# Linear attention in front of two MLPs on one core: k and v of a head pair in one gapless load each

## The chip, the core and the metric

The kernel runs on one core of a Trainium2 chip. A core has five engines that run side by side and wait for each other by semaphores: TensorE (PE in the rows; its loads of the stationary operand are listed apart as PEld), VectorE (DVE), ScalarE (ACT), GpSimd (POOL) and SyncE (SP), which here only issues transfers. The transfers of all issuers run on the same 16 DMA engines. The metric is the time of one execution on the device, in microseconds.

## What is computed

```python
def _attn_ref(q, k, v, g_norm):                       # 4 x 8 heads, 576 rows, 64 columns
    kv = np.einsum('bhsd,bhse->bhde', k, v)           # 64 x 64 per head
    out = np.einsum('bhsd,bhde->bhse', q, kv)
    rms = np.sqrt(np.mean(out * out, axis=-1, keepdims=True) + 1e-06)
    return out / rms * g_norm
...
x = attn_out.transpose(0, 2, 1, 3).reshape(2304, 512)
h = x @ w_in            # 512 x 2048, then softplus, then @ w_out
...
h = x @ w_in2           # the same sizes, then leaky relu (0.01), then @ w_out2
```

k^T v of a head is a sum over all 576 rows, so the order in which the rows are taken doesn't matter as long as k and v are taken alike. All inputs and the output are float32.

## The kernel before

**Work and its order.** The 32 heads are taken as 16 units of two heads each (`unit`, four head pairs in each of four batches). Each step of the program is an `op` with a price for each engine that may do it; `Plan.run` gives every op an engine and a place in that engine's queue, at build time. The first 600 or so places are not planned but written out by hand in the table `FIRST` (a letter for the engine, E for TensorE, G for a transfer that ScalarE issues, and the number of the op); what follows the table is ordered by prices and due times. Each engine then works through its queue in order.

**Loads (`load`, L430).** For each unit q, k and v are loaded with 512 of their 576 rows, four rows of a head to a partition: 128 partitions x 2 heads x 256 elements, 256 KB, in runs of 1 KB. There are five buffers of each (`qa`, `ka`, `va`). The 64 rows that are left come once a batch for all heads: `kr` and `vr` with 64 partitions x 8 heads x 64, and `qr` in two halves. Those of the first batch are issued by ScalarE, the others by SP. The lower halves of `kr` and `vr` are set to zero once, on GpSimd, so that they can be multiplied with all 128 partitions.

**A unit (`T`, L460).** q and k are copied with the two heads side by side (`qp`, `kp`, L406 to L410, on ScalarE, VectorE or GpSimd). TensorE turns q in four transposes (`f_t`, L479; at the first unit of two also the left rows of q, L483), and multiplies k with v: four products of 128 x 128 over the rows (`f_kv`, L487) and a fifth over the left rows (`f_kvl`, L492). Both heads stand in k and in v, so a product of 128 columns holds the two wanted 64 x 64 blocks and two that are not wanted; a mask takes the blocks out (`f_m`, L505 on VectorE, L508 on ScalarE) into `kvm`. A product in fp32 is two loads of weights and two passes, as two records in the trace.

**Behind it.** `O` (L523) multiplies the turned q with `kvm` (L527, and L534 for the left rows of two units), `normal` (L558) makes the norm, `X` (L606) turns the result back (L612, L623) into `xy`. In between stand the decoding of the first MLP weights (`decode_pair`, `split_pair`) and the first plain products of the MLP (L984). The MLPs (L894, L1151, L1156 and what feeds them) fill the rest.

Of the kernel before, what the change touches and what calls it, by code (L numbers as in the profile page):

```python
# [21 lines left out]
class Plan:  # L22
# [13 lines left out]
    S7 E26 S0 S80 G6 S9 G5 S8 S1 G4 P40 S2 G3 D27 S85 E44 E42 S10 E32 S13 A82 S14 S15 A83 S11 A81 E29  # L36
    S24 D41 S12 D30 E45 S23 D28 D84 S38 S16 A90 E33 A31 S37 S19 E34 E46 D35 S39 D47 A36 D91 E69 A43 S17
    D87 E52 A88 S20 D48 D55 A86 E68 S18 A53 D89 P100 S22 A72 D54 A70 E102 S21 P101 E104 A92 D73 E57 D71
    S50 E60 E105 A58 S49 D103 A74 P56 D59 S51 A75 E106 D76 E61 S66 A107 D25 D78 S65 A108 E62 D79 E134
    S67 D77 A63 S110 D93 A64 E132 S109 A136 P166 E135 E116 A167 D94 P119 D95 A138 E168 D139 A117 D137  # L40
    E170 E171 A133 D118 P120 A169 E124 D96 A140 E172 E178 D97 A141 A173 E125 D142 A174 D145 A98 D144
    E126 E180 S131 E121 D127 E200 A179 D143 S129 P185 S113 A128 D186 A122 E198 D99 A123 S115 E182 A202
    P213 A199 S114 D181 E187 D203 A183 E201 S146 P212 E190 A204 E191 S111 D184 A321 S130 D205 D188 E192
    A206 S112 P236 E214 D189 E228 A207 D208 E216 P235 S175 A229 E217 S151 D211 D209 A215 A193 S176 E218
    E230 P262 D219 S177 E248 A194 D210 A231 E232 A324 S195 D220 S196 D322 E251 S197 E250 A254 A249 D325
    S222 E266 S245 A252 E264 E274 S225 D265 A233 E237 D255 D253 A147 E240 S227 E481 P263 A238 D234 S226
    A148 D149 E241 S221 A256 D150 P281 A257 S223 A275 E242 D258 S246 E267 A156 D261 S224 A243 D259 A239
# [120 lines left out]
def linear_attention_two_mlps(  # L168
# [32 lines left out]
    nc = tc.nc  # L201
# [178 lines left out]
    for t_ in ldr["k"] + ldr["v"]:  # L380
        nc.gpsimd.memset(t_[RL:], 0.0)
# [48 lines left out]
    def load(u):  # L430
        b, hp = unit(u)
        hs = slice(2 * hp, 2 * hp + 2)
        for nm, src in (("q", q), ("k", k), ("v", v)):
            def fn(e, nm=nm, src=src):
                nc.sync.dma_start(
                    out=lda[nm][u % NLD],
                    in_=src[b, hs, 0:4 * P, :].rearrange("h (p r) d -> p h r d", r=4),
                )

            op({"S": 0.73}, fn, (), [(nm, u % NLD)])  # L440
        if u % NPAIR:
            return
        e_ = "G" if b == 0 else "S"
        for nm, src in (("k", k), ("v", v)):
            def fn(e, nm=nm, src=src):
                (nc.scalar if e == "G" else nc.sync).dma_start(
                    out=ldr[nm][b % 2][:RL], in_=src[b, :, 4 * P:S, :].rearrange("h p d -> p h d")
                )

            op({e_: 0.58}, fn, (), [(nm + "r", b % 2)])  # L450
        for x in range(2):
            def fn(e, x=x):
                (nc.scalar if e == "G" else nc.sync).dma_start(
                    out=ldr["q"][b % 2][x * RL:(x + 1) * RL],
                    in_=q[b, NPAIR * x:NPAIR * (x + 1), 4 * P:S, :].rearrange("h p d -> p h d"),
                )

            op({e_: 0.29}, fn, (), [("qr", b % 2, x)])

    def T(u):  # L460
# [3 lines left out]
        for nm, dst in (("q", qp), ("k", kp)):  # L464
# [6 lines left out]
        kv = ps[p1][:, 2 * P:3 * P]  # L471
        ql, kl, vl = (ldr[nm][b % 2] for nm in "qkv")
# [4 lines left out]
        def f_t(e, j):  # L477
# [16 lines left out]
        for j in range(2):  # L494
            n = 2 * P
            op(
                {"PE": 0.22 if i or j else 0.33}, lambda e, j=j: f_t(e, j),
                [("qp", i)] + ([] if i or j else [("qr", b % 2, x) for x in range(2)]), [("ps", p0 + j)],
            )
            if j:  # L500
                op({"PE": 0.88}, f_kv, [("kp", i), ("v", u % NLD)], [("ps", p1)])
                op({"PE": 0.22}, f_kvl, [("kr", b % 2), ("vr", b % 2)], [("ps", p1)])
                def f_m(e):
                    if e == "D":
                        nc.vector.tensor_tensor(kvm_, kv, mask, ALU.mult)  # L505
                        return
                    for h in (slice(0, D), slice(D, P)):
                        nc.scalar.activation(  # L508
                            kvm_[:, h], kv[:, h], AF.Copy, scale=mask[:, h.start:h.start + 1]
# [4 lines left out]
            if i == j == 0:  # L514
# [745 lines left out]
    for i in range(NU + XL):  # L1260
        if i in (3, 5):
            plan.AHEAD = 14.0
            decode_pair(2 * (i == 5), 0, 0)
            split_pair(0, int(i == 5), True)
# [20 lines left out]
       + [(t, i) for t in ("qp", "kp", "qtl") for i in range(2)] + [("kvm", i) for i in range(4)]  # L1285
       + [("qt", i, j) for i in range(2) for j in range(2)]
       + [(t, i) for t in "qkv" for i in range(NLD)]
       + [(t + "r", i) for t in "kv" for i in range(2)]
# [109 lines left out]
```

## Time and profile before

| | us |
|---|---|
| median of 3 runs | 782.07 (780.84 to 782.99) |
| profiled execution, its time | 784.06 |
| profiled execution, span of the instructions | 782.1 |
| TensorE busy in the span | 767.8 |
| VectorE busy | 679.3 |
| ScalarE busy | 544.2 |

The profile is of one execution, which took 784.06 us, so a sum made from its rows is compared with that time and not with the median. Busy time counts an instruction from its start to its end, also where TensorE's products overlap. A row of the timeline gives start, duration, engine, line, operation, what is written and read, and how many like instructions are merged in the row; in brackets stands the time for which the engine was idle before it and what ended that.

### The profile page before, as it was taken

To read this page: it belongs to the slowest core of one execution; us is meant where nothing else is said; L and a number is where in the kernel's file an instruction comes from. 1 tells how busy PE (TensorE), PEld (TensorE's weight loads), DVE (VectorE), ACT (ScalarE), POOL (GpSimd) and SP (SyncE) were. 2 spreads that over 40 slices of the span, in tenths; PEclk is the share of its full clock that TensorE was granted. 3 is DMA by queue.
4 is the path that set the end of the run, shared out by engine and by line. 5 is a ranking of instruction groups with operands and counts; after the bars stand their busy time and mean duration, and the time that the engine had idled before them with its cause. 6 is when DMAs were issued, how large, how long until landed. Compare 5 with 4: busy or idle time off the path is not lost.

```text
span 782.1 us, 13225 instructions
## 1 busy us (share of the span) xinstructions
PE 767.8 (98%) x5029; PEld 763.6 (98%) x5029; DVE 679.3 (87%) x1084; ACT 544.2 (70%) x930; POOL 20.9 (3%) x37
## 2 busy tenths in 40 slices
PE   6899999999999999999999999999999999999997
PEld 6899999999999999999999999999999999999997
DVE  3999999999899897996899999998899877886666
ACT  4789999788676775764588788885677645554441
POOL 2330000000000000000000000000000000000000
PEclk8999999999999999999999999999999999999999
DMA  9995768685784794683678969785875772562814
GB/s 284 289 312 166 288 225 308 248 295 200 307 321 166 266 340 150 264 304 106 255 279 293 332 213 414 306 301 193 315 268 180 279 253 104 210 246 102 299 41 122
DMA packets 80416, 192.50 MB, mean 246 GB/s; under 512 B 11616, under 2 KB 54624, under 8 KB 80352
## 3 DMA queue, kind: packets, MB, share of 16 engines
q1 hardware_dynamic: 77136, 190.47, 67.8%
q10 hardware_dynamic: 3216, 1.18, 0.6%
q8 instruction: 40, 0.66, 0.3%
q14 instruction: 24, 0.20, 0.1%
HBM read 152.31 MB, written 39.32 MB: 245 GB/s over the span
## 4 chain that ended last, share of the span: by engine, by line
PE 92%; DVE 4%; DMA 3%; issue 0%; SPq 0%; ACT 0%; DVEq 0%
PE ps L894 41%; PE ps L1151 23%; PE ps L1156 20%; PE ps L984 2%; PE ps L487 2%; PE ps L527 1%; DMA xscr<-rc 1%; DMA ka<-in_k_dram 1%; PE ps L612 1%; DMA ra<-xscr 1%; PE ps L479 1%; DVE xy L774 1%; DVE ra L740 0%; PE ps L534 0%; PE ps L492 0%
## 5 line engine op out<-in xcount | busy, mean ns | idle before, releaser
L894 PE MATMUL ps<-ra 128*128 128x384 f32 x1932 | 385.1, 335 | 0.7 <-DMA ra<-xscr 0.7
L894 PEld LDWEIGHTS ps<-ra 128*128 128x128 f32 x1932 | 332.0, 188 | 1.0 <-DMA ra<-xscr 1.0
L1151 PE MATMUL ps<-rb 128*128 128x256 f32 x1512 | 203.9, 282 | 0.0
L1156 PE MATMUL ps<-rb 128*128 128x384 f32 x1008 | 200.4, 334 | 0.0
L1151 PEld LDWEIGHTS ps<-rb 128*128 128x128 f32 x1512 | 198.0, 189 | 0.1
L923 ACT ACTIVATE rb<-mf 128x768 fp32r<-128x768 f32 x154 | 129.9, 846 | 69.5 <-PE ps L1151 39.0
L1156 PEld LDWEIGHTS ps<-rb 128*128 128x128 f32 x1008 | 177.0, 188 | 0.0
L928 DVE TENSOR_TENSOR rb<-mf,rb 128x768 fp32r<-128x768 f32 x154 | 146.7, 954 | 23.7 <-ACT rb L923 22.5
L774 DVE TENSOR_TENSOR xy<-ps,xy 128x384 f32<-128x384 f32 (+2 forms) x247 | 134.7, 549 | 32.5 <-PE ps L1151 22.0
L1008 DVE TENSOR_TENSOR mf<-mf 128x768 f32<-128x768 f32 x68 | 64.2, 953 | 2.4 <-ACT mf L909 1.8
L1201 ACT ACTIVATE mf<-ps 128x384 f32<-128x384 f32 x92 | 44.7, 489 | 30.2 <-PE ps L894 28.5
L1208 DVE TENSOR_TENSOR mf<-ps,mf 128x384 f32<-128x384 f32 x92 | 50.8, 554 | 11.6 <-PE ps L894 10.3
L1213 ACT ACTIVATE ps<-ps 128x384 f32<-128x384 f32 x46 | 22.0, 479 | 21.0 <-PE ps L894 20.9
L909 ACT ACTIVATE mf<-mf 128x768 f32<-128x768 f32 x26 | 21.9, 846 | 17.2 <-DVE mf L1208 17.0
L1073 DVE TENSOR_TENSOR rb<-rc,rb 128x512 fp32r<-128x512 f32 x44 | 29.7, 683 | 0.0
L1070 ACT ACTIVATE rb<-rc 128x512 fp32r<-128x512 f32 x44 | 27.5, 626 | 1.7 <-PE ps L1151 0.8
L915 ACT ACTIVATE mf<-mf 128x768 f32<-128x768 f32 x24 | 20.1, 839 | 9.6 <-DVE mf L1208 9.6
L1167 ACT ACTIVATE ps<-ps 128x384 f32<-128x384 f32 (+2 forms) x44 | 21.0, 479 | 7.1 <-PE ps L1156 4.3
L676 ACT ACTIVATE sqr<-mf 128x512 f16<-128x512 f32 x23 | 18.2, 790 | 7.2 <-DMA kr<-in_k_dram 6.8
L915 ACT ACTIVATE mf<-ps 128x384 f32<-128x384 f32 x32 | 15.7, 490 | 9.6 <-PE ps L894 9.4
L487 PE MATMUL ps<-va,kp 128*128 128x128 f32 x128 | 18.6, 294 | 3.5 <-DVE kp L408 3.5
L687 ACT ACTIVATE sqr<-mf 128x512 uint16<-128x512 uint16 x28 | 21.9, 783 | 0.0
(123 smaller groups left out, 747.0 us busy)
## 6 DMA issues: line engine op xcount, KB each, us to landing
ra<-xscr SPq DMA_DIRECT2D x131, 768.0 KB, 6.3
xscr<-ra SPq DMA_DIRECT2D x30, 768.0 KB, 4.9
mf<-in_moe_w_in_dram SPq DMA_DIRECT2D x18, 512.0 KB, 6.1
mf<-in_moe_w_out_dram SPq DMA_DIRECT2D x18, 512.0 KB, 6.1
lf<-in_moe_w_in_dram SPq DMA_DIRECT2D x14, 512.0 KB, 6.0
lf<-in_moe_w_out_dram SPq DMA_DIRECT2D x14, 512.0 KB, 5.1
xscr<-xy SPq DMA_DIRECT2D x8, 768.0 KB, 5.7
qa<-in_q_dram SPq DMA_DIRECT2D x16, 256.0 KB, 5.0
```

Of the source, the lines that this page charges most:

```text
L487: nc.tensor.matmul(kv, kp[i][:, r, :, :], va[:, :, r, :], start=(r == 0), stop=False)
L774: {"D": t_d(n)}, lambda e: nc.vector.tensor_tensor(dst, src, dst, ALU.add),
L894: nc.tensor.matmul(o, w_[:, a, c:c + P], e_[:, b, kk, :], start=(not on and which < 2 and kk == 0 and n == 0), stop=(kk == 1 and n == 2), ...
L915: lambda e: nc.scalar.activation(dst(), src(), AF.Prelu, alpha=0.01),
L923: {"A": t_a(n)}, lambda e: nc.scalar.activation(g[:, 0, :, :], c.ap, AF.Copy),
L928: lambda e: nc.vector.tensor_tensor(g[:, 1, :, :], c.ap, g[:, 0, :, :].bitcast(F32), ALU.subtract),
L1008: lambda e: nc.vector.tensor_tensor(to.ap, x.ap, y.ap, ALU.subtract),
L1073: lambda e: nc.vector.tensor_tensor(w_[:, 1], src(), w_[:, 0].bitcast(F32), ALU.subtract), sk + hk, lk,
L1151: nc.tensor.matmul(y[:, 256 * (j % 2):256 * (j % 2 + 1)], G_[:, a, m, js], w_[:, b, m, :], **flags)
L1156: nc.tensor.matmul(y[:, :BN], w_[:, a, m, js], G_[:, b, m, :], **flags)
L1201: {"A": t_a(BN)}, lambda e: nc.scalar.activation(c[:, m, :], src, AF.Copy),
L1208: lambda e: nc.vector.tensor_tensor(c[:, m, :], src, c[:, m, :], ALU.add),
```

## The change

k and v of a unit are loaded in one transfer each with all 576 rows: a partition takes nine successive rows of one head (2304 bytes in one run), the first head on partitions 0 to 63 and the second on 64 to 127. The separate loads of the left rows of k and v, their buffers and their products (`f_kvl`) go. Since the two heads now stand on different partitions, k is copied into `kp` in two halves of 64 partitions, each into the columns of its head, and the other columns stay zero, set once on GpSimd. A product has k between zeros as its stationary operand, 128 columns wide, and 64 columns of v; there are nine of them, and the 64 columns that come out hold the first head's block over the second's. The mask spreads them over 128 columns. q is loaded as before; its left rows are turned with the second unit of two in place of the first, and all their transfers are issued by SP. The decoding of the second part of the first weights moves from step 5 to step 9 of the loop, and the table `FIRST` is new throughout.

```diff
     FIRST = """
-    S7 E26 S0 S80 G6 S9 G5 S8 S1 G4 P40 S2 G3 D27 S85 E44 E42 S10 E32 S13 A82 S14 S15 A83 S11 A81 E29
+    E22 S0 S5 S1 S2 S6 S7 A23 S4 P35 E28 S19 E26 S3 A25 D24 E41 S8 E29 S11 A37 D36 S9 S20 A30 E42 S10
...
-    lda = {nm: ring(attp, nm + "a", NLD, [P, 2, 4, D]) for nm in "qkv"}
-    ldr = {nm: ring(attp, nm + "r", 2, [P, H // (2 if nm == "q" else 1), D]) for nm in "qkv"}
+    NR = S // RL
+    lda = {nm: ring(attp, nm + "a", NLD, [P, 2, 4, D] if nm == "q" else [P, NR, D]) for nm in "qkv"}
+    ldr = {"q": ring(attp, "qr", 2, [P, H // 2, D])}
...
-    kp = ring(attp, "kp", 2, [P, 4, 2, D])
+    kp = ring(attp, "kp", 2, [P, NR, 2, D])
...
-    for t_ in ldr["k"] + ldr["v"]:
-        nc.gpsimd.memset(t_[RL:], 0.0)
+    for t_ in kp:
+        for x in range(2):
+            nc.gpsimd.memset(t_[x * RL:(x + 1) * RL, :, 1 - x, :], 0.0)
...
+                if nm == "q":
+                    in_ = src[b, hs, 0:4 * P, :].rearrange("h (p r) d -> p h r d", r=4)
+                else:
+                    in_ = src[b, hs, :, :].rearrange("h (p r) d -> (h p) r d", r=NR)
+                nc.sync.dma_start(out=lda[nm][u % NLD], in_=in_)
...
-        for nm, src in (("k", k), ("v", v)):
-            def fn(e, nm=nm, src=src):
-                (nc.scalar if e == "G" else nc.sync).dma_start(
-                    out=ldr[nm][b % 2][:RL], in_=src[b, :, 4 * P:S, :].rearrange("h p d -> p h d")
-                )
...
+        for x in range(2):
             copy_to(
-                dst[i], lda[nm][u % NLD].rearrange("p h r d -> p r h d"), 512,
-                [(nm, u % NLD)], [(nm + "p", i)], "AD" if u == 0 else "ADP",
+                kp[i][x * RL:(x + 1) * RL, :, x, :], lda["k"][u % NLD][x * RL:(x + 1) * RL], NR * D,
+                [("k", u % NLD)], [("kp", i, x)], engines,
             )
...
-            if j == 0 and i == 0:
+            if j == 0 and i == 1:
                 nc.tensor.transpose(ps[p0][:, 2 * P:3 * P], ql[:, lq, :], ident)
...
-            for r in range(4):
+            for r in range(NR):
                 nc.tensor.matmul(
-                    kv, kp[i][:, r, :, :], va[:, :, r, :], start=(r == 0), stop=False
-                )
-
-        def f_kvl(e):
-            nc.tensor.matmul(kv, kl[:, h2, :], vl[:, h2, :], start=False, stop=True)
+                    kv, kp[i][:, r, :, :], va[:, r, :], start=(r == 0), stop=(r == NR - 1)
+                )
...
-                        nc.vector.tensor_tensor(kvm_, kv, mask, ALU.mult)
+                        nc.vector.tensor_tensor(
+                            kvm_.rearrange("p (h d) -> p h d", h=2), kv[:, None, :].to_broadcast([P, 2, D]),
+                            mask.rearrange("p (h d) -> p h d", h=2), ALU.mult,
+                        )
...
-        if i in (3, 5):
+        if i in (3, 9):
             plan.AHEAD = 14.0
-            decode_pair(2 * (i == 5), 0, 0)
-            split_pair(0, int(i == 5), True)
+            decode_pair(2 * (i == 9), 0, 0)
+            split_pair(0, int(i == 9), True)
```

How the queues stand at three places follows; a number behind a name is that of the buffer.

The queue of SP at its start, in the kernel before (`mf` takes the first MLP weights, 512 KB an issue):

```order
L435 DMA qa1_99<-in_q_dram 128x2x256
L435 DMA qa0_98<-in_q_dram 128x2x256
L647 DMA mf_76<-in_moe_w_in_dram 128x4x256
L435 DMA va1_109<-in_v_dram 128x2x256
L435 DMA ka1_104<-in_k_dram 128x2x256
L435 DMA ka0_103<-in_k_dram 128x2x256
L435 DMA va0_108<-in_v_dram 128x2x256
L647 DMA mf_76<-in_moe_w_in_dram 128x4x256
```

Beside it ScalarE issues the two halves of `qr` and then `vr` and `kr`. The same place after the change:

```order
L442 DMA qa0_98<-in_q_dram 128x2x256
L442 DMA qa1_99<-in_q_dram 128x2x256
L442 DMA ka0_103<-in_k_dram 128x576
L442 DMA va0_108<-in_v_dram 128x576
L442 DMA ka1_104<-in_k_dram 128x576
L442 DMA va1_109<-in_v_dram 128x576
L449 DMA qr0_113<-in_q_dram 64x4x64
```

The weights, which stood third and eighth, now stand 17th and 20th, and k and v of the first unit follow q directly. ScalarE issues nothing.

The queue of TensorE at the first two units, before (`ps` are banks of PSUM, `qp` and `kp` the copies, `qt` and `qtl` the turned q):

```order
L479 MATMUL ps0_84<-ident_60,qp0_119 128x128 x2
L483 MATMUL ps0_84<-ident_60,qr0_113 128x128
L487 MATMUL ps3_87<-va1_109,kp1_122 128x128 x4
L487 MATMUL ps1_85<-va0_108,kp0_121 128x128 x4
L492 MATMUL ps1_85<-vr0_117,kr0_115 128x128
L492 MATMUL ps3_87<-vr0_117,kr0_115 128x128
L534 MATMUL ps6_90<-kvm0_127,qtl0_125 128x128
L534 MATMUL ps6_90<-kvm1_128,qtl0_125 128x128
L527 MATMUL ps4_88<-kvm0_127,qt0_123 128x128 x4
L527 MATMUL ps5_89<-kvm1_128,qt1_124 128x128 x4
```

And after the change:

```order
L488 MATMUL ps1_85<-va0_108,kp0_117 128x64 x9
L488 MATMUL ps3_87<-va1_109,kp1_118 128x64 x9
L480 MATMUL ps2_86<-ident_60,qp1_116 128x128 x2
L484 MATMUL ps2_86<-ident_60,qr0_113 128x128
L528 MATMUL ps4_88<-kvm0_123,qt0_119 128x128 x4
L528 MATMUL ps5_89<-kvm1_124,qt1_120 128x128 x4
L480 MATMUL ps0_84<-ident_60,qp0_115 128x128 x2
L480 MATMUL ps2_86<-ident_60,qp1_116 128x128 x2
L484 MATMUL ps2_86<-ident_60,qr0_113 128x128
L535 MATMUL ps6_90<-kvm0_123,qtl0_121 128x128
L535 MATMUL ps6_90<-kvm1_124,qtl0_121 128x128
```

Four wide products and one for the left rows became nine narrow ones in a row; the left rows of q are turned behind them, and L535 now stands directly behind the second such transpose.

The queue of GpSimd behind its memsets, before (`qp` and `kp` are written from the loaded q and k):

```order
L410 TENSOR_SCALAR qp1_120<-qa1_99 128x512
L410 TENSOR_SCALAR qp1_120<-qa3_101 128x512
L410 TENSOR_SCALAR kp1_122<-ka3_106 128x512
L410 TENSOR_SCALAR kp0_121<-ka2_105 128x512
L410 TENSOR_SCALAR qp1_120<-qa0_98 128x512
L410 TENSOR_SCALAR qp0_119<-qa4_102 128x512
```

And after the change, from the place where its halves come in pairs:

```order
L413 TENSOR_SCALAR qp0_115<-qa1_99 128x512
L413 TENSOR_SCALAR kp0_117<-ka1_104 64x9x64 x2
L413 TENSOR_SCALAR qp1_116<-qa2_100 128x512
L413 TENSOR_SCALAR kp1_118<-ka2_105 64x9x64 x2
L413 TENSOR_SCALAR qp0_115<-qa3_101 128x512
```

GpSimd has 11 whole copies of k before and 24 half copies after the change, and 14 and 12 copies of q; VectorE and ScalarE make the rest.

## Rows read from the trace of the kernel before

**Rows 1.** The page: busy us of each engine, share of the span, count.

```profile
PE 767.8 (98%) x5029; PEld 763.6 (98%) x5029; DVE 679.3 (87%) x1084; ACT 544.2 (70%) x930; POOL 20.9 (3%) x37
```

**Rows 2.** Stretches: length; busy us of PE, PEld, DVE, ACT, POOL; clock, DMA share, GB/s.

```profile
0.00:25.00 25.00, 16.99 (x114) 16.22 (x115) 12.48 (x33) 11.09 (x26) 7.45 (x19) 0.86 0.94 287
25.00:62.00 37.00, 36.41 (x304) 34.84 (x303) 34.53 (x80) 31.28 (x79) 13.45 (x18) 1.00 0.90 276
62.00:430.00 368.00, 367.17 (x2143) 365.67 (x2142) 335.51 (x519) 282.06 (x470) 0.04 (x1) 1.00 0.70 254
430.00:782.10 352.10, 347.22 (x2474) 346.90 (x2472) 296.82 (x455) 219.73 (x359) 0.00 (x0) 1.00 0.64 232
...
7.74:14.57 6.83, 3.66 (x17) 3.66 (x18) 1.79 (x4) 2.48 (x5) 0.00 (x0) 0.50 1.04 333
```

**Rows 3.** Timeline of the first 25 us, TensorE and VectorE: start, duration, instruction, idle before.

```profile
4.42 0.43 DVE L408 COPY qp<-qa 128x512 f32<-128x512 f32 x1 [2.94 <-DMA qa<-in_q_dram]
...
7.15 0.30 PE L483 MATMUL ps<-ident,qr 128*128 128x128 f32 x1 [1.58 <-DMA qr<-in_q_dram]
...
10.43 0.43 DVE L408 COPY kp<-ka 128x512 f32<-128x512 f32 x1 [5.58 <-DMA ka<-in_k_dram]
...
10.91 3.78 PE L487 MATMUL ps<-va,kp 128*128 128x128 f32 x16 [3.46 <-DVE kp L408]
...
14.48 0.65 PE L492 MATMUL ps<-vr,kr 128*128 128x128 f32 x4
...
22.73 1.13 PE L527 MATMUL ps<-kvm,qt 128*128 128x128 f32 x8 [1.66 <-DVE xn L590]
```

**Rows 4.** The chain of waits in order of time: start, us, what.

```profile
3.02 7.38 DMA ka<-in_k_dram
```

**Rows 5.** Chain of waits, a unit's products; then timeline, loads of one unit.

```profile
42.51 0.89 PE ps L487 x8
43.40 0.22 PE ps L492 x2
...
25.80 0.97 PEld L487 LDWEIGHTS ps<-va,kp 128*128 128x128 f32 x8
```

**Rows 6.** Timeline in narrow stretches: the first load, and the first two, after a wait.

```profile
22.70 0.19 PEld L527 LDWEIGHTS ps<-kvm,qt 128*128 128x128 f32 x1 [1.82 <-ACT qt L420]
...
22.70 0.30 PEld L527 LDWEIGHTS ps<-kvm,qt 128*128 128x128 f32 x2 [1.82 <-ACT qt L420]
...
37.13 0.14 PEld L612 LDWEIGHTS ps<-ident,xn 128*128 128x128 f32 x1 [0.52 <-ACT qt L420]
...
37.13 0.20 PEld L612 LDWEIGHTS ps<-ident,xn 128*128 128x128 f32 x2 [0.52 <-ACT qt L420]
```

**Rows 7.** DMA issues of the first 25 us: count, KB each, median us to landing.

```profile
ka<-in_k_dram SPq DMA_DIRECT2D x8, 256.0 KB, 4.9
mf<-in_moe_w_in_dram SPq DMA_DIRECT2D x2, 512.0 KB, 5.9
qr<-in_q_dram ACTq DMA_DIRECT2D x2, 64.0 KB, 4.3
vr<-in_v_dram ACTq DMA_DIRECT2D x1, 128.0 KB, 7.1
```

**Rows 8.** Groups of instructions to 95 us, GpSimd's copies: busy us, mean ns.

```profile
L410 POOL TENSOR_SCALAR qp<-qa 128x512 f32<-128x512 f32 x14 | 9.8, 708 | 33.3 <-PE ps L492 10.6 <-PE ps L483 6.3 <-DMA qa<-in_q_dram 5.3
L410 POOL TENSOR_SCALAR kp<-ka 128x512 f32<-128x512 f32 x11 | 8.4, 760 | 7.0 <-DMA ka<-in_k_dram 3.4 <-PE ps L487 2.0 <-PE ps L612 0.8
```

**Rows 9.** Timeline of VectorE and GpSimd, 20 to 28 us.

```profile
20.00 0.27 DVE L422 COPY qtl<-ps 128x128 f32<-128x128 f32 x1
...
20.42 1.21 POOL L410 TENSOR_SCALAR qp<-qa 128x512 f32<-128x512 f32 x2 [2.59 <-DVE qtl L422]
20.47 0.59 DVE L578 SCALAR_TENSOR_TENSOR fm<-ss,fa 128x18 f32<-128x18 f32 x1 [0.20 <-ACT fa L573]
...
27.71 0.18 DVE L578 SCALAR_TENSOR_TENSOR fm<-ss,fa 128x18 f32<-128x18 f32 x1
```

More of the change, by code (lines that the diff above doesn't have):

```diff
@@ L456, in fn @@
                 )
[L458 removed]
+            op({"S": 0.29}, fn, (), [("qr", b % 2, x)])
     def T(u):
@@ L463, in T @@
         i = u % 2
-        for nm, dst in (("q", qp), ("k", kp)):
+        engines = "AD" if u == 0 else "ADP"
+        copy_to(
+            qp[i], lda["q"][u % NLD].rearrange("p h r d -> p r h d"), 512,
+            [("q", u % NLD)], [("qp", i)], engines,
+        )
+        for x in range(2):
             copy_to(
-                dst[i], lda[nm][u % NLD].rearrange("p h r d -> p r h d"), 512,
-                [(nm, u % NLD)], [(nm + "p", i)], "AD" if u == 0 else "ADP",
+                kp[i][x * RL:(x + 1) * RL, :, x, :], lda["k"][u % NLD][x * RL:(x + 1) * RL], NR * D,
+                [("k", u % NLD)], [("kp", i, x)], engines,
             )
@@ L470, in T @@
         p1 = p0 + 1
-        kv = ps[p1][:, 2 * P:3 * P]
-        ql, kl, vl = (ldr[nm][b % 2] for nm in "qkv")
+        kv = ps[p1][:, 2 * P:2 * P + D]
+        ql = ldr["q"][b % 2]
         lq = slice(2 * (hp % 2), 2 * (hp % 2) + 2)
@@ L496, in T @@
             op(
-                {"PE": 0.22 if i or j else 0.33}, lambda e, j=j: f_t(e, j),
-                [("qp", i)] + ([] if i or j else [("qr", b % 2, x) for x in range(2)]), [("ps", p0 + j)],
+                {"PE": 0.33 if i and not j else 0.22}, lambda e, j=j: f_t(e, j),
+                [("qp", i)] + ([("qr", b % 2, x) for x in range(2)] if i and not j else []), [("ps", p0 + j)],
             )
             if j:
-                op({"PE": 0.88}, f_kv, [("kp", i), ("v", u % NLD)], [("ps", p1)])
-                op({"PE": 0.22}, f_kvl, [("kr", b % 2), ("vr", b % 2)], [("ps", p1)])
+                op({"PE": NR * 0.12}, f_kv, [("kp", i, 0), ("kp", i, 1), ("v", u % NLD)], [("ps", p1)])
                 def f_m(e):
                     if e == "D":
-                        nc.vector.tensor_tensor(kvm_, kv, mask, ALU.mult)
+                        nc.vector.tensor_tensor(
+                            kvm_.rearrange("p (h d) -> p h d", h=2), kv[:, None, :].to_broadcast([P, 2, D]),
+                            mask.rearrange("p (h d) -> p h d", h=2), ALU.mult,
+                        )
                         return
@@ L508, in f_m @@
                         nc.scalar.activation(
-                            kvm_[:, h], kv[:, h], AF.Copy, scale=mask[:, h.start:h.start + 1]
+                            kvm_[:, h], kv, AF.Copy, scale=mask[:, h.start:h.start + 1]
                         )
@@ L513, in T @@
             from_psum(qt[i][:, j * n:(j + 1) * n], ps[p0 + j][:, :n], n, p0 + j, [("qt", i, j)])
-            if i == j == 0:
+            if i and not j:
                 ql_ = qtl[u // 2 % 2].rearrange("p (a n) -> p a n", n=RL)[:, ::2, :]
@@ L1284, in linear_attention_two_mlps @@
     op({"N": 0.0}, attention_done, (), granules("rb")
-       + [(t, i) for t in ("qp", "kp", "qtl") for i in range(2)] + [("kvm", i) for i in range(4)]
+       + [(t, i) for t in ("qp", "qtl") for i in range(2)] + [("kp", i, x) for i in range(2) for x in range(2)] + [("kvm", i) for i in range(4)]
        + [("qt", i, j) for i in range(2) for j in range(2)]
        + [(t, i) for t in "qkv" for i in range(NLD)]
-       + [(t + "r", i) for t in "kv" for i in range(2)]
        + [("qr", i, x) for i in range(2) for x in range(2)])
```

56 lines of the change are left out of this document (26 added, 30 removed).

## Prediction

> **What bounds the kernel now.** I read the busy table first, then the table of stretches, then the timeline of the first 25 us, and last the single loads and products of TensorE. TensorE is busy for 767.8 of 782.1 us [rows 1], so the end moves only if TensorE gets less or more to do, or starts or waits otherwise. The stretches show where it waits at all [rows 2]: it is idle for 8.0 us of the first 25 us (25.00 less 16.99), for 0.59 us from 25 to 62, for 0.83 us in all the stretch from 62 to 430, and for 4.9 us behind that, in the tail. The change touches the attention alone, which lies ahead of 80 us. What it can win by shorter waits is therefore bounded by some 9 us, and from 25 us on every added TensorE microsecond is a microsecond of the end.
>
> The largest of the waits in the head are [rows 3] 1.58 us for the left rows of q, 3.46 us for the first k, and 1.66 us at 22.7 us. The first k\*v product starts at 10.91, after a DVE copy at 10.43, which waited for a k transfer issued at 3.02 and 7.38 us long [rows 3, 4]. So the head is bound by transfers: the sixteen DMA engines are 94% busy there [rows 2].
>
> **The change part by part.**
>
> *The products (the large term).* A unit (two heads) now has five 128-column products for k\*v, four of L487 and one of L492. Each is two loads of weights and two passes, so ten pairs: 0.89 us for eight and 0.22 us for two, 1.11 us in all, 0.11 us a pair [rows 5]. After the change it has nine products of 64 columns, eighteen pairs, with a full 128-column stationary operand in each (k between zeros). No product of 64 columns stands in the trace, so the price of a pair is bounded from both sides. If the columns set it, half the columns take half of 0.11 us, 0.055 us. If the load of the weights sets it, the nearest rows are loads that follow each other while the array has nothing else to do: at 22.70 TensorE had been idle for 1.66 us, and one load takes 0.19 us and two take 0.30 us, so the second starts 0.11 us after the first although no product was in its way [rows 6]. The loads of transposes show that this is a property of the load: there two take 0.20 us and one 0.14 us, 0.06 us apart [rows 6]. In before this is hidden, since a pass of 128 columns lasts as long as the load of the next weights; a pass of 64 columns would not hide it. I take 0.11 us, because these rows are of the same kind of load (fp32, 128 columns, not a transpose) and the lower end has no row of its own. Eighteen at 0.11 us are 1.98 us, 0.87 us more than 1.11, and over 16 units **+13.9 us**. At 0.055 us they are 0.99 us, 0.12 us less, -1.9 us over 16 units.
>
> [...]
>
> *The head.* Before, between the landing of the first q at 4.42 and that of the first k at 10.40, the queues carry 512 KB of weights, a v, two k (768 KB) and the left rows, two of q of 64 KB and one each of v and k of 128 KB: 1664 KB in 6.0 us, 278 KB a us [rows 3, 4, 7]. Now the weights and q's left rows come later, the left rows of k and v are within the loads, and behind the two q stand the k and v of unit 0, 2 x 288 KB. At that rate they take 2.1 us and v lands at 6.5; k's two half copies are done before. The first product starts at 6.6 in place of 10.91, **-4.3 us**. The next k and v take another 2.1 us, to 8.6, which is when 1.98 us of products end: from there on a unit's loads (about 3 us) are shorter than a unit's TensorE work, so the wait of 1.66 us at 22.7 us goes, less about half a microsecond, **-1.2 us**. That half is the copy of q's turned left rows (0.27 us [rows 9] and its way to and fro), which in the first pair now stands between its transpose and L535; in later pairs k\*v and q products lie between. [...]
>
> *Copies and memsets.* k comes in two copies of 64 partitions x 576 in place of one of 128 x 512; GpSimd makes 24 of the halves in place of 11 whole ones. At 0.76 us for 512 [rows 8] a half is 0.86 us; with q's copies that is at most 2.4 us a unit, less than a unit of TensorE, and k is loaded units ahead, so I cost it at nothing; if the cover went, a unit would wait for 0.86 us more. The zeros in kp are four memsets of the old count, 576 in place of 512 wide, ahead of the first q. The mask on DVE keeps its 128 columns, and its first operand is read twice.
>
> *Moves.* The eight transposes of q's left rows stay eight and go to odd units. Of the four transfers that ScalarE issued, the two of q's left rows go to SP, and the two of k and v vanish, as six do on SP. The second quarter of the first weights is decoded at step 9 in place of 5; its products then stand later on TensorE, where there is no idle time to win or lose [rows 2]. I set the new order behind the attention at 0, with 0.8 us either way, the idle time from 62 to 430.
>
> **Sum.** 13.9 - 4.3 - 1.2 = **+8.4 us**. The profiled execution took 784.06 us, 2.0 us above the median of 782.07 us; against it the sum is 792.5, and on the median **790.5 us**. Its own range is 786 to 795: with loads 0.104 us apart (0.11 is rounded: eighteen are 1.87 us, +12.2 us), all 6.0 us of the two waits and the cheap clock, +4.5; with 0.11 us, 3 us of the waits and the dear clock, +12.8.
>
> **The rivals.**
>
> *The columns set the pace (other side, faster).* If a load of weights can overlap the one before it, a pair takes 0.055 us and the products give 1.9 us. Then not TensorE but the transfers are next: the bytes of k and v are the same, and DMA is 94% and 90% busy to 62 us [rows 2], so of the 4.3 us of the head about half stays. -1.9 - 2.1 = -4.0, **778 us**, between 776 and 782. For it speaks that in a chain eight loads take 0.97 us [rows 5], 0.11 us apart like the passes, so that such rows can't tell which of the two sets the pace. Against it stands the second of two loads that met an idle array. It decides from a pair below 0.09 us.
>
> *Loads overlap in part.* The array may hide some of a load in the one before: halfway, 0.083 us, eighteen are 1.49 us, +6.1 us, and less 5.5 us for the waits **782.7 us**. [...]
>
> *GpSimd holds DVE up.* In 25 to 62 us DVE is busy for 34.53 of 37 us [rows 2]. Beside two GpSimd copies at 20.42 a DVE step takes 0.59 us that takes 0.18 us at 27.71 [rows 9]; 13 more copies at 0.41 us are 5.3 us, 2.8 us over DVE's 2.5 us of room. This decides only where TensorE isn't longer anyway, thus with the cheap pair: 778 + 2.8 = **781 us**; it needs seven such meetings. In the forecast DVE gets 14 us of room and it costs nothing. [...]
>
> **How the numbers follow.** Forecast 0.73, columns 0.14, partial overlap 0.07, GpSimd 0.06. A measurement of this kernel can tell about 0.3% (2.3 us) from no change. Slower: 0.73 and 0.02 of the partial overlap, 0.75. Faster: 0.11 of the columns and 0.01 of GpSimd, 0.12. Same: 0.05 + 0.05 + 0.03, 0.13. The range is 779 to 795: it leaves out a tenth of the forecast and half of the columns, about 0.15 in all.
>
> **What would show it.** In the profile after, eighteen pairs of L488 in about 2.0 us with the loads 0.11 us apart, right; 1.0 us, wrong, and the first rival is the case. First L488 at 6 to 7.5 us. The first block of L895 about 8 us later than the first of L894 before. TensorE idle in the first 25 us 3 us rather than 8. The stretch from 100 us on of the old length, only later. The forecast falls if consecutive loads of L488 start nearer than 0.09 us, or if the head wins more than 6 us.

## The result and the profile after

| | before | after |
|---|---|---|
| median, us | 782.53 (780.84 to 783.12) | 792.71 (792.32 to 794.74) |
| profiled execution, its time | 784.06 | 793.03 |
| span | 782.1 | 791.2 |

The ratio of after to before is 1.0139, with an interval of 1.0115 to 1.0163: the kernel became 10.2 us slower. The forecast was 790.5 us, its range 779 to 795. The two profiled executions are 9.0 us apart; the one of before lay 1.5 us over its median, that of after 0.3 us.

The page of after, busy time and the group of the new loads (the first row answers to [rows 1]):

```profile
PE 782.8 (99%) x5157; PEld 779.4 (99%) x5157; DVE 682.6 (86%) x1087; ACT 545.0 (69%) x929; POOL 30.7 (4%) x48
...
L488 PEld LDWEIGHTS ps<-va,kp 128*128 128x128 f32 x288 | 34.8, 199 | 3.7 <-ACT kp L409 2.2
```

The stretches of after (columns as in [rows 2]; the last row is the part at the lower clock):

```profile
0.00:25.00 25.00, 21.70 (x139) 20.99 (x140) 10.97 (x30) 11.15 (x24) 7.71 (x19) 0.86 0.93 308
25.00:62.00 37.00, 35.97 (x320) 35.12 (x320) 30.13 (x69) 27.91 (x66) 18.77 (x24) 1.00 0.79 262
62.00:430.00 368.00, 367.78 (x2174) 366.60 (x2174) 335.04 (x522) 277.13 (x467) 4.22 (x5) 1.00 0.67 246
430.00:791.20 361.20, 357.32 (x2530) 356.71 (x2528) 306.45 (x469) 228.83 (x374) 0.00 (x0) 1.00 0.65 234
...
10.23:17.05 6.82, 6.82 (x34) 6.82 (x34) 2.34 (x7) 2.14 (x7) 0.67 (x1) 0.50 0.97 309
```

The timeline of after, TensorE, in the head and at later units, and the loads of one unit (start, duration, instruction, idle before):

```profile
4.63 1.49 PE L480 MATMUL ps<-ident,qp 128*128 128x128 f32 x6
7.92 5.82 PE L488 MATMUL ps<-va,kp 128*128 128x64 f32 x36 [1.81 <-DMA va<-in_v_dram]
...
13.96 0.42 PE L484 MATMUL ps<-ident,qr 128*128 128x128 f32 x1
14.18 3.32 PE L528 MATMUL ps<-kvm,qt 128*128 128x128 f32 x16
...
17.88 0.61 PE L535 MATMUL ps<-kvm,qtl 128*128 128x128 f32 x4
...
23.02 1.16 PE L528 MATMUL ps<-kvm,qt 128*128 128x128 f32 x8 [0.17 <-DVE xn L591]
...
24.88 0.68 PE L535 MATMUL ps<-kvm,qtl 128*128 128x128 f32 x4 [0.26 <-ACT sq L549]
...
27.28 2.09 PEld L488 LDWEIGHTS ps<-va,kp 128*128 128x128 f32 x18
...
43.64 2.12 PE L488 MATMUL ps<-va,kp 128*128 128x64 f32 x18
...
46.03 2.12 PE L488 MATMUL ps<-va,kp 128*128 128x64 f32 x18
...
52.04 2.22 PE L488 MATMUL ps<-va,kp 128*128 128x64 f32 x18 [0.66 <-POOL kp L413]
...
61.16 2.22 PE L488 MATMUL ps<-va,kp 128*128 128x64 f32 x18 [0.34 <-POOL kp L413]
```

The chain of waits of after: the transfer of the first v, which stands where k's stood in [rows 4], and one unit's products, which answer to the two rows of [rows 5]:

```profile
2.25 5.54 DMA va<-in_v_dram
...
27.55 1.96 PE ps L488 x18
```

The stretch in which that v landed (columns as in [rows 2]):

```profile
4.50:7.92 3.42, 1.62 (x8) 1.24 (x8) 0.74 (x1) 0.68 (x1) 0.41 (x1) 1.00 1.01 322
```

And from the kernel before, TensorE behind its first k\*v products:

```profile
15.38 0.68 PE L534 MATMUL ps<-kvm,qtl 128*128 128x128 f32 x4 [0.25 <-DVE kvm L505]
15.90 1.95 PE L527 MATMUL ps<-kvm,qt 128*128 128x128 f32 x16
```

TensorE has 15.0 us more to do (782.8 less 767.8) and waits 5.9 us less, 8.4 against 14.3; that is the 9.1 us of the span. Of the 15.0 us, 13.6 are the products: 1.96 us in place of 0.89 and 0.22, 0.85 us more in each of 16 units. The other 1.4 us are the sixteen products of L528 at 14.18, which take 3.32 us where L527 took 1.95 in the kernel before: now it is they that lie in the stretch with the granted clock at 0.50. Of the idle time, 4.7 us went in the first 25 us (3.30 in place of 8.01), 0.4 us came from 25 to 62, 0.6 us went from 62 to 430 and 1.0 us in the tail.

### The profile page after: what moved, and what is told of

It is laid out like the page before. It is cut to its first block, busy times and chain, and to the rows that moved or that the text cites. A ratio compares the mean times of both kernels' runs of the same rounds, so it can differ in the third digit from the quotient of the medians.

```text
span 791.2 us, 13489 instructions
## 1 busy us (share of the span) xinstructions
PE 782.8 (99%) x5157; PEld 779.4 (99%) x5157; DVE 682.6 (86%) x1087; ACT 545.0 (69%) x929; POOL 30.7 (4%) x48
## 4 chain that ended last, share of the span: by engine, by line
PE 94%; DMA 2%; DVE 1%; issue 1%; POOL 1%; ACT 0%; SPq 0%; DVEq 0%; POOLq 0%
PE ps L895 41%; PE ps L1152 23%; PE ps L1157 21%; PE ps L488 4%; PE ps L985 2%; PE ps L528 2%; DMA ra<-xscr 1%; DMA xscr<-xy 1%; POOL kp L413 1%; DMA va<-in_v_dram 1%; PE ps L480 1%; PE ps L613 1%; PE ps L535 0%; SPq L442 0%; DVE xn L591 0%
## 5 line engine op out<-in xcount | busy, mean ns | idle before, releaser
L895 PE MATMUL ps<-ra 128*128 128x384 f32 x1932 | 385.5, 335 | 0.5 <-DMA ra<-xscr 0.5
L895 PEld LDWEIGHTS ps<-ra 128*128 128x128 f32 x1932 | 332.0, 188 | 0.9 <-ACT ps L1168 0.8
L488 PEld LDWEIGHTS ps<-va,kp 128*128 128x128 f32 x288 | 34.8, 199 | 3.7 <-ACT kp L409 2.2
L488 PE MATMUL ps<-va,kp 128*128 128x64 f32 x288 | 35.6, 281 | 2.8 <-DMA va<-in_v_dram 1.8
L688 ACT ACTIVATE sqr<-mf 128x512 uint16<-128x512 uint16 x29 | 22.7, 782 | 0.0
```

The lines of the kernel that those rows point to most:

```text
L488: nc.tensor.matmul(kv, kp[i][:, r, :, :], va[:, r, :], start=(r == 0), stop=(r == NR - 1))
L895: nc.tensor.matmul(o, w_[:, a, c:c + P], e_[:, b, kk, :], start=(not on and which < 2 and kk == 0 and n == 0), stop=(kk == 1 and n == 2), ...
```

## Experiments

Each was timed beside the kernel before, whose median there was 781.31 to 781.92 us; the ratios are to that. The changed kernel was not timed again with them, so against it (1.0139) the ratios say more than the medians.

### What a pair of load and pass costs

**Half as many stationary columns.** The two heads one after the other, each with its own 64 columns of `kp`: 36 pairs a unit, the contraction over 128 partitions as before.

```diff
-            for r in range(NR):
-                nc.tensor.matmul(kv, kp[i][:, r, :, :], va[:, r, :], ...)
+            for x in range(2):
+                for r in range(NR):
+                    nc.tensor.matmul(kv[x * D:(x + 1) * D], kp[i][:, r, x, :], va[:, r, :], ...)
```

> Each of the nine products of a unit is split into two whose stationary operand is 64 columns wide (one head's columns with the zeros of the other head's rows), each with the same 64 columns of v: 36 pairs of load and pass a unit in place of 18. Theory (the load of the weights sets the pace of a 64-column product, and it grows with the stationary columns): a load of 64 columns takes half, so the pairs stand about 0.056 us apart, a unit takes about 2.0 us, and the whole is 792.7 us as after the change, within 2 us. Rival (a pass has a floor of its own of about 0.11 us, whatever the load): 36 x 0.11 = 4.0 us a unit, 2.0 us more in 16 units, about 825 us.

790.80 us, ratio 1.0121 (1.0100 to 1.0141).

**Twice as many moving columns.** Eight of the nine products take 128 columns of v, two rows of the head; what the second half yields isn't used.

```diff
-                    kv, kp[i][:, r, :, :], va[:, r, :], ...
+                    ps[p1][:, 2 * P:2 * P + n * D], kp[i][:, r, :, :], va[:, r:r + n, :], ...
```

> As after the change, but eight of the nine products move 128 columns of v (the wanted 64 and 64 that are not used) past the same stationary operand. Theory (load sets the pace): the pairs stay 0.11 us apart, a unit takes 2.0 us and the whole 792.7 us, within 1.5 us, so that the narrower pass had bought nothing. Rival (the columns or a cost per column of the pass set the pace of after): 64 columns more cost up to 0.05 us a pair, 16 x 16 x 0.05 = 13 us, about 805 us.

789.23 us, ratio 1.0100 (1.0080 to 1.0121).

**Quarter tiles.** Each head multiplied in its own quarter, its 64 partitions by its 64 columns, the two heads in turn:

```diff
             for r in range(NR):
-                nc.tensor.matmul(kv, kp[i][:, r, :, :], va[:, r, :], ...)
+                for x in range(2):
+                    s_ = slice(x * RL, (x + 1) * RL)
+                    nc.tensor.matmul(kv[s_], kp[i][s_, r, x, :], va[s_, r, :], ...)
```

> As after the change, but each product is split by head: 64 partitions x 64 stationary columns of k against 64 partitions x 64 columns of v, the two heads on different rows and columns of the array, so that the zeros are not multiplied. 36 pairs a unit. Theory (loads set the pace): at half the columns a load takes 0.056 us, so 2.0 us a unit and 792.7 us if the loads of the two heads follow each other; if the array takes the load of one head beside the pass or load of the other, down to 1.0 us a unit, 16 us less, 777 us. Rival (a floor of the pass of 0.11 us): 4.0 us a unit one behind the other, 825 us, or 2.0 us and 792.7 us if two run side by side.

782.92 us, ratio 1.0016 (1.0005 to 1.0028). The timelines of the three kernels in this order, one unit each (half loads by their loads, the others by their products):

```profile
14.68 2.00 PEld L489 LDWEIGHTS ps<-va,kp 128*64 128x64 f32 x36 [0.19 <-DVE kp L411]
```

```profile
14.67 2.19 PE L489 MATMUL ps<-va,kp 128*128 128x128 f32 x18
```

```profile
15.31 1.26 PE L490 MATMUL ps<-va,kp 64*64 64x64 f32 x36
```

In a unit of the half loads 36 loads of 64 columns fill the time of 18 loads of 128 columns (2.00 us against 2.09; from start to start 53 ns on the mean, 2.00 us less one load of 0.14 over 35, against 111 to 112): the pass has no floor of its own near 0.11 us, and the load sets the pace by its columns. Passes of 128 columns take the same 2.19 us for 18 pairs as those of 64 (2.12 or 2.22): the narrower pass bought nothing. So the choice of 0.11 us is shown from both sides. The times alone would not show it: by the ratios the half loads are 1.4 us under the changed kernel, within the intervals, and the wide passes 3.1 us, more than the 1.5 us that their theory allowed. In both profiles the granted clock is 1.00 from 5 us to 780 us; what a stretch at 0.50 costs is priced below.

The quarter tiles halve what is left: where two successive loads lie in different partitions and columns, the two take 58 ns together (a row cut off behind 20 of a unit's products is 0.80 us long, all 36 take 1.26 us). In the changed kernel 18 loads of 128 rows, beside passes on the same rows, keep their pace when the passes get twice as wide (2.12 and 2.19 us). Rows and columns are not separated here: the quarters of the two heads differ in both.

### The head

**The weights early again.** The changed kernel with the two weight transfers back at the third and eighth place of SP's list:

```diff
-    E22 S0 S5 S1 S2 S6 S7 A23 S4 ...
+    E22 S0 S5 S75 S1 S2 S6 S7 S80 A23 S4 ...
```

> The changed kernel, of which only SP's list is altered: the two issues of 512 KB of MLP weights stand third and eighth again, as in the kernel before. It is the counterpart of the run that delays them in the kernel before. Theory (the head's gain of 3.0 us comes from the place of the weights and from the left rows that vanished, about 1.8 us of it from the weights): the first L488 starts near 9.7 in place of 7.92, and the time is 1 to 2 us over the changed kernel, 793.7 to 794.7; a longer empty stretch ahead of the first product may add as much again if the clock falls for longer. Rival (the left rows alone gave it): the first L488 within 0.5 us of 7.92, time unchanged.

795.73 us, ratio 1.0176 (1.0156 to 1.0197), 3.0 us over the changed kernel. Its timeline and the stretch at the lower clock:

```profile
9.79 7.49 PE L488 MATMUL ps<-va,kp 128*128 128x64 f32 x36 [3.67 <-DVE kp L411]
```

```profile
10.27:20.50 10.23, 10.23 (x51) 10.23 (x51) 3.00 (x8) 2.80 (x8) 0.67 (x1) 0.50 0.97 321
```

The first product starts 1.87 us later, the 1.8 us that 512 KB cost at the rate of [rows 3, 4, 7]. The rest comes by the clock: at the lower level TensorE is busy for 10.23 us in place of 6.82, and half of the 3.4 us more is lost, 1.7 us. Together 3.6 us; the first block of L895 stands 3.5 us later (102.00 in place of 98.52). So of the 3.0 us by which the change starts its products sooner, 1.87 come from the place of the weights alone.

**The weights late in the kernel before.** The counterpart: both weight issues behind k and v of the first two units. The second, eighth in the list, stands there already, so one issue moves and nothing else.

```diff
-    S7 E26 S0 S80 G6 S9 G5 S8 S1 G4 P40 S2 G3 D27 S85 E44 ...
+    S7 E26 S0 G6 S9 G5 S8 S1 G4 P40 S2 G3 D27 S80 S85 E44 ...
```

> The kernel before the change, of which only SP's list is altered: the two issues of 512 KB of MLP weights, which stand third and eighth there, go behind the four issues of k and v of the first two units. Theory (the head is bound by transfers, and the weights among k and v cost what their bytes cost): 512 KB ahead of the first k at 278 KB a us are 1.8 us, so the first L487 starts near 9.1 in place of 10.91 and the time is 1 to 2 us under the kernel before, near 779.5 to 780.5. Rival (the weights are needed by then: their decoding and the first plain products come later and TensorE waits for them): the first L487 comes earlier, but a wait of 1 us or more appears behind it, and the time is that of the kernel before or longer. Rival 2 (transfers share their engines, so that the order of issue matters little): the first L487 stays within 0.5 us of 10.91.

782.61 us, ratio 1.0007 (0.9994 to 1.0020). The timelines of TensorE and of ScalarE:

```profile
8.48 3.78 PE L487 MATMUL ps<-va,kp 128*128 128x128 f32 x16 [1.63 <-DVE kp L408]
...
14.69 1.22 PE L534 MATMUL ps<-kvm,qtl 128*128 128x128 f32 x4 [1.58 <-ACT qtl L420]
15.71 3.04 PE L527 MATMUL ps<-kvm,qt 128*128 128x128 f32 x16
```

```profile
11.40 0.78 ACT L676 ACTIVATE sqr<-mf 128x512 f16<-128x512 f32 x1 [9.39 <-DMA kr<-in_k_dram]
...
14.06 0.42 ACT L748 ACTIVATE ra<-mf 128x256 fp32r<-128x256 f32 x1 [0.76 <-DVE mf L701]
14.38 0.26 ACT L420 ACTIVATE qtl<-ps 128x128 f32<-128x128 f32 x1
```

The same steps of ScalarE in the kernel before:

```profile
8.86 0.78 ACT L676 ACTIVATE sqr<-mf 128x512 f16<-128x512 f32 x1 [6.84 <-DMA kr<-in_k_dram]
...
12.66 0.26 ACT L420 ACTIVATE qtl<-ps 128x128 f32<-128x128 f32 x1
```

The first product came 2.4 us sooner, and the time didn't fall: the sign of the first rival. By the rows two things took the gain, about as much each. In ScalarE's queue the decoding of the first weights (L676 to L748) stands ahead of the copy `qtl`, so that weights that land later (L676 2.5 us later) push `qtl` from 12.66 to 14.38, and L534 waits 1.58 us for it. And the granted clock, which in this profile is at 0.50 for 10.24 us, makes L534 and the sixteen L527 4.26 us long in place of 2.63. To tell the one from the other, the same kernel with eight products of zeros ahead of the first product:

```diff
+            if u == 1:
+                for _ in range(8):
+                    nc.tensor.matmul(ps[7][:, 0:P], idle, idle, start=True, stop=True)
```

> The kernel before the change with the two weight transfers behind k and v of the first two units, as in the run that did this alone, and eight products of zeros on TensorE ahead of the first k*v product. There the first L487 had started 2.4 us sooner, the idle time of the first 25 us had fallen by 2.5 us, and the time had not: in its profile the granted clock was 0.50 for 10.24 us in place of 6.83, so that the 20 loads of k*v, the four of L534 and the sixteen of L527 took twice as long. Theory (the lower clock took back what the transfers gave): with the clock kept at its upper level, no row of 0.50 behind 8 us, the time falls to 779 to 780.5, about 2 us under that run's 782.61. Rival (the weights that come later are what took it back): the time stays within 0.7 us of 782.6, with waits of 1 us or more behind the first products whatever the clock.

781.96 us, ratio 1.0003 (0.9988 to 1.0018). Its timeline, and the stretch at the lower clock:

```profile
8.56 2.19 PE L490 MATMUL ps<-va,kp 128*128 128x128 f32 x16
12.25 0.71 PE L495 MATMUL ps<-vr,kr 128*128 128x128 f32 x4 [1.50 <-DMA kr<-in_k_dram]
14.57 1.22 PE L537 MATMUL ps<-kvm,qtl 128*128 128x128 f32 x4 [1.61 <-ACT qtl L420]
```

```profile
13.18:20.00 6.82, 5.43 (x25) 5.43 (x26) 5.33 (x11) 3.84 (x10) 1.98 (x3) 0.50 1.02 332
```

The first sixteen loads ran at the upper level, 2.19 us in place of 3.78, and then TensorE waited for the left rows of k and again for `qtl`, 3.1 us in all. The clock fell all the same, behind the first of these waits, so the condition of the theory (no stretch at 0.50) wasn't met. What the run does show is that the wait for `qtl` is there also where the first loads run at the upper level; how much of the loss is the clock's stays open. Why the changed kernel keeps its gain I only read from the queues: the left rows of k and v come within the loads there, and the decoding stands later in ScalarE's queue too. No run tests that.

### The stretch at the lower clock

**The changed kernel, with filler.** Twelve products of zeros ahead of the first product of unit 0, in the manner of the last diff.

> As after the change, with twelve products of zeros (128 columns, 24 pairs, 2.7 us at full clock) put in front of the first k*v product, where TensorE waits from 5.6 to 7.9 us. Theory (the granted clock of 0.50 from 10.2 to 17.1 us follows the idle stretch before it, and the loads run at that clock): the clock stays at 1.00, the 26 pairs that took 0.21 us take 0.11 us and what lies behind them too, 3 to 4 us less, some 0.4 us of filler on the path, about 789.5 us. Rival (the clock falls all the same, or the transfers bind the first 20 us): 792.7 to 793.2 us.

790.48 us, ratio 1.0121 (1.0104 to 1.0138), 2.2 us less than the changed kernel by the medians, 1.4 by the ratios, whose intervals overlap; 3 to 4 were expected.

**The kernel before, with filler.** Fifteen such products ahead of unit 1, the first there:

> The kernel before the change with 15 products of zeros on TensorE ahead of the first k*v product, and nothing else changed. It prices the stretch of 6.83 us at the lower clock that the prediction put at 1.7 us. Theory (half the clock costs the difference of what lies in it, 17 pairs at 0.10 us): the first L487 stays near 10.9, the clock stays at its upper level, and the time falls by 1.5 to 2 us, to about 780. Rival (behind it TensorE waits for transfers that end as late as ever, 1.66 us at 22.7 us among them, so that what the clock gives goes into that wait): the stretch vanishes and the time stays within 0.7 us of the kernel before.

780.33 us, ratio 0.9982 (0.9972 to 0.9992), 1.5 us less. Timelines of the first and of the second:

```profile
5.91 2.96 PE L489 MATMUL ps<-xy 128*128 128x128 f32 x24
8.71 4.13 PE L491 MATMUL ps<-va,kp 128*128 128x64 f32 x36
...
13.01 1.95 PE L531 MATMUL ps<-kvm,qt 128*128 128x128 f32 x16
```

```profile
7.54 3.51 PE L488 MATMUL ps<-xy 128*128 128x128 f32 x30
11.10 2.33 PE L490 MATMUL ps<-va,kp 128*128 128x128 f32 x16
...
20.52 1.13 PE L530 MATMUL ps<-kvm,qt 128*128 128x128 f32 x8 [0.70 <-DVE xn L593]
```

In both profiles the granted clock is 1.00 from 7.3 us to 776 us. In the changed kernel the 36 pairs take 4.13 us in place of 5.82 and the sixteen products of `O` 1.95 in place of 3.32, 3.1 us in all, of which the fillers cost 0.8 by holding the first product until 8.71; that leaves 2.3. In the kernel before, sixteen loads take 2.33 us in place of 3.78, and the wait at 22.7 us [rows 3] is still 0.70 us long. So by the rows the stretch costs about 1.5 us in the kernel before, which the time bears out, and about 3 us in the changed one, where the time is less sure. What speaks against the larger figure: one of the four executions of the changed kernel had a mean clock of 1.000 and took 794.74 us; why that one wasn't shorter stays open. In the quarter tiles from copies six of ten executions had a mean clock of 0.999 or 1.000 and four 0.996 or 0.997; their medians are 782.4 and 783.5 us, and their ranges overlap.

### The half copies

**Quarter tiles straight from the loaded k.** With a head in its own quarter no zeros are needed, and so no copy of k. (The step stays in the list, empty; two of the loads of k stand at another place in SP's queue.)

```diff
-                        kv[s_], kp[i][s_, r, x, :], va[s_, r, :], ...
+                        kv[s_], ka[s_, r, :], va[s_, r, :], ...
...
-    for t_ in kp:
-        for x in range(2):
-            nc.gpsimd.memset(t_[x * RL:(x + 1) * RL, :, 1 - x, :], 0.0)
...
-            copy_to(kp[i][x * RL:(x + 1) * RL, :, x, :], lda["k"][u % NLD][x * RL:(x + 1) * RL], ...)
+            op({e: 0.02 for e in engines}, lambda e: None, [("k", u % NLD)], [("kp", i, x)])
```

> The changed kernel with products of 64 partitions x 64 columns straight from the loaded k, two heads in the two opposite quarters of the array, 36 loads and passes a unit; k isn't copied at all, there are no zeros and no halves for GpSimd. The same products read from the copies gave 782.92 us, 1.26 us a unit and 2.3 us of idle time from 25 to 62 us, which ended on GpSimd's halves of k. Theory (the halves are a cost of the change that the prediction set at nothing, and it is the waits for them that keep the quarter tiles from winning): 1.26 us a unit stay, the idle time from 25 to 62 us falls below 1 us, the first product starts some 0.4 us sooner, and the time is 1.5 to 3 us under that of the quarter tiles from copies, 780 to 781.5. Rival (TensorE waits for the transfers or for q's copies, which end little later): the idle time stays near 2 us, ended by another engine or by DMA, and the time stays within 1 us of 782.9.

778.86 us, ratio 0.9957 (0.9946 to 0.9968): faster than both kernels, and 1.1 us below what the theory allowed. The stretch from 25 to 62 us, first of the quarter tiles from copies, then of these (ahead of it their first product):

```profile
25.00:62.00 37.00, 35.13 (x526) 31.76 (x528) 35.39 (x76) 30.38 (x74) 21.98 (x29) 1.00 0.77 274
```

```profile
7.43 1.26 PE L490 MATMUL ps<-va,ka 64*64 64x64 f32 x36 [1.77 <-DMA va<-in_v_dram]
...
25.00:62.00 37.00, 37.00 (x556) 34.43 (x552) 34.69 (x85) 32.61 (x79) 5.28 (x9) 1.00 0.81 282
```

Without the copies the quarter tiles' idle time from 25 to 62 us went from 1.87 us (37.00 less 35.13) to nothing, and GpSimd's work from 21.98 to 5.28 us. But not all of the 1.87 us had ended on the halves, as the expectation has it (with 2.3 us). From copies, the rows give the halves 0.53 us at 45.08 and 0.21 at 52.48; 0.70 at 33.91, and 0.63 at the edge of the stretch, ended on VectorE's `xnl`:

```profile
33.91 0.33 PE L627 MATMUL ps<-ident,xnl 128*128 128x128 f32 x1 [0.70 <-DVE xnl L594]
...
45.08 1.26 PE L490 MATMUL ps<-va,kp 64*64 64x64 f32 x36 [0.53 <-POOL kp L413]
```

A step of VectorE ahead of that `xnl`, in the stretch in which GpSimd is busy for 21.98 us of 37; then the same step without the copies, where it is busy for 5.28:

```profile
32.94 0.52 DVE L584 SCALAR_TENSOR_TENSOR fm<-fm,fa 128x18 f32<-128x18 f32 x1
```

```profile
31.52 0.18 DVE L584 SCALAR_TENSOR_TENSOR fm<-fm,fa 128x18 f32<-128x18 f32 x1
```

The step takes 0.52 us and 0.18 us. That is the sign of the prediction's third rival (GpSimd holds VectorE up), where the prediction said it would count, with cheap pairs. VectorE also lost half copies of its own in the run without copies, so the two are not separated.

The timeline of GpSimd in the changed kernel shows how it came to hold TensorE up:

```profile
48.30 3.68 POOL L413 TENSOR_SCALAR kp<-ka 64x576 f32<-64x576 f32 x4 [5.22 <-issue]
...
57.54 3.57 POOL L413 TENSOR_SCALAR kp<-ka 64x576 f32<-64x576 f32 x4 [4.20 <-PE ps L488]
```

Four halves, those of two units, stand in a row there, 3.6 to 3.7 us, and TensorE, which needs the eleventh unit next (`kp0`), waits for the last of them. GpSimd's queue at 48.30 has them in this order:

```order
L413 TENSOR_SCALAR kp1_118<-ka1_104 64x9x64 x2
L413 TENSOR_SCALAR kp0_117<-ka0_103 64x9x64 x2
```

The halves of the twelfth unit stand first, and `kp1` comes free only with the tenth unit's products, at 48.15 (46.03 and 2.12 us; "issue" in the row means that it names nothing that ended the wait). `kp0` had been free since 45.76 (43.64 and 2.12), but its halves stand behind. At 57.54 the order is the same. So the wait comes from the order in the hand-written table, together with the two buffers of `kp`. With the eleventh unit first, its two halves (half of 3.68 us) would by these rows be done by 47.6, ahead of the 51.4 at which TensorE begins to wait; that is an estimate, and no run has that order.

The same with nine products of zeros in front:

> The quarter tiles straight from the loaded k, with nine products of zeros in front of the first product, on TensorE alone. In the changed kernel such products kept the granted clock at its upper level from 6.14 us on and gave 2.2 us. Theory (a stretch at the lower level behind an almost idle head costs what lies in it): no row of clock 0.50 behind 7 us, and 1 to 2 us less than without them, 778.5 to 780.5, which is under the kernel before as well. Rival (with the short products there is little TensorE work in that stretch, and the next unit's transfers end as late as ever): within 0.7 us of the run without them.

778.77 us, ratio 0.9961 (0.9947 to 0.9976), thus the rival's result. But its ground isn't tested: in the profile of the kernel without the fillers the granted clock is 1.00 from 5.07 us to 776 us as well, so there was nothing to win.

## Why the prediction was right, and where its sizes were off

- **The products**, +13.9: right. 13.6 us by the chain's rows, with loads 111 to 112 ns apart. The two runs with half as wide loads and twice as wide passes show that the load of the stationary operand is the cause, not the pass. The first rival and the partial overlap are out; both needed a pair of under 0.09 us.
- **The head**, -4.3: mis-sized. The first product starts at 7.92, not 6.6, -3.0 us. The mechanism holds: moving 512 KB of weights moves that start by 1.87 us in the changed kernel and by 2.4 in the one before. What failed is the arrival of v, which the step put at 6.5 and which landed at 7.79 (2.25 and 5.54 us). The transfers were not slower than the rate taken, 278 KB a us: from 4.50 to 7.92 they ran at 322 GB/s, some 1.1 MB, where the unit's k and v are 0.58 MB. So transfers behind them in the list moved beside them, and the step, which let v land as soon as the bytes ahead of it were through, left those out.
- **The wait at 22.7 us**, -1.2: right in size, in part by luck. The 1.66 us before L527 became 0.17 at 23.02 and 0.26 before L535 at 24.88, -1.2 us. But the half microsecond that the step kept was for the copy of q's left rows ahead of the first L535, and no wait is there: between their transpose at 13.96 and L535 at 17.88 stand the sixteen L528, and the transpose directly ahead of L535 is that of the next pair. What is left waits for `xn` and `sq`.
- **The clock**, 0, and in the range a cheap clock at -1.7 and a dear one at +1.9: mis-sized too, on the other side. No run shows the two terms as such; in their place the runs show a stretch at 0.50 in both kernels, which the filler runs price at 1.5 us before and 3 us after. It kept its length of 6.8 us, but TensorE was busy through all of it, 6.82 us against 3.66 in [rows 2], and the sixteen products of `O` fell into it: +1.4 us.
- **GpSimd's halves**, at nothing: wrong by 1.0 us. TensorE waited 0.66 and 0.34 us for them at 52 and 61 us. The step said that k is loaded units ahead, and took that for the cover; but the copies wait for `kp` as well, and twice the halves that are needed first stand behind a pair that must wait for later products. The step's own price of a lost cover, 0.86 us a unit, was met in part, twice.
- **The moves**, 0 with 0.8: right within their range from 62 to 430 us, where 0.22 us of idle time stand in place of 0.83. That the tail lost 1.0 us was not foreseen. The first block of L895 stands at 98.52, 10.8 us behind L894's 87.75, where 8 were expected; the list too is another one there.

In all TensorE's work grew by 15.0 us where 13.9 were expected, and its waits fell by 5.9 where 5.5 were. Against its own profiled execution the sum gave 792.5 us, and 793.03 came; on the medians the two kernels lie another 1.2 us apart, since the profiled execution of before was above its median by more than that of after. That the waits come so near is partly luck: the first 25 us gave back 4.7 and not 5.5, 0.4 came from 25 to 62 us, and 1.6 went behind 62 us, where the prediction had set nothing.

## What to carry to other kernels

Where every product brings its own weights and moves no more columns than it loads (here fp32, 128 loaded, 64 or 128 moved), count the columns of the stationary operand and not those of the moving one: zeros in it cost as much as data (18 loads with zeros 2.09 us and eight without 0.97 us [rows 5], 111 to 112 ns apart in both), and cutting the pass in half wins nothing (18 pairs in 2.12 or 2.22 us with 64 columns, in 2.12 or 2.19 with 128). Two operands that need only their own block go into opposite quarters of the array, which here took 36 loads in 1.26 us where 18 full ones took 2.1, and needed neither zeros nor copies. Before a transfer is moved back in a queue, look at what uses its data on the other engines: a late decoding ahead of an urgent copy took up to 1.6 us of the 2.4 us gained here. And where an engine fills two buffers in turn, let it fill first the one that is needed first.

## What the runs showed of the hardware

The spacing of loads went with the clock: at 0.50 ten loads of 128 columns take 2.25 us in the changed kernel, 213 ns apart, where eighteen take 2.09 us at 1.00, 111 to 112 ns apart. In the kernel before, twelve of the loads that go with the first products of [rows 3] take 2.68 us at 0.50 (from 11.29), 213 ns apart too. Their passes have 128 columns, those of the changed kernel 64, so the spacing went with the load and not with the pass.

```profile
10.87 2.25 PEld L488 LDWEIGHTS ps<-va,kp 128*128 128x128 f32 x10
```

The clock did not follow from the list of instructions. In the profiles of the half loads, the wide passes and the tiles without copies the granted clock is 1.00 from about 5 us on (to 776 or 780 us) without filler; in that of the changed kernel it is 0.50 from 10.23 to 17.05 us, 0.86 over the first 25 us, and in that of the quarter tiles from copies it is 0.93 over the first 25 us, though the list is the same but for the k\*v products and the copies of k. Nor did the kernel alone decide it: executions of the changed kernel had a mean clock of 0.996 or of 1.000, those of the quarter tiles from copies 0.996 to 1.000. What tips it was not tried.
